# Decode attention over two layers: each batch row through both layers in turn, part of its V kept in SBUF, 0.5 MB chunks

## Chip, cores, metric

The kernel runs on one core of a Trainium2 chip. The time is that of the whole execution on the device, in microseconds; lower is better. PE is the matmul engine, PEld its weight loads, DVE VectorE, ACT ScalarE, SP the engine that issues the DMAs.

## The reference

Four batch rows with one query token each go through attention over a KV cache, an FFN, and both again with the same weights and the same cache. There are 32 query heads, 8 KV heads, 8192 keys, head size 128, model width 512, FFN width 1792, all bf16.

```python
def attention(x, k_cache, v_cache, wq, wo):       # k_cache, v_cache: [4, 8, 8192, 128]
    q = (x @ wq)...                               # [4, 32, 1, 128]
    scores = einsum("bhqd,bhkd->bhqk", q, k) * 128 ** -0.5
    return einsum("bhqk,bhkd->bhqd", softmax(scores), v)... @ wo
def ffn(x, w_gate, w_up, w_down):
    return (silu(x @ w_gate) * (x @ w_up)) @ w_down
x = x + attention(layernorm(x)); x = x + ffn(layernorm(x))
x = x + attention(layernorm(x)); x = x + ffn(layernorm(x))
```

K and V are 67.1 MB each, and both layers read both: 268.4 MB. The weights are 13.9 MB. Nearly all of the work is to read the cache.

## The kernel before

All four rows go through layer 1 together, then through layer 2. A K chunk is 1 MB: 1024 keys of one KV head for the four rows. PE transposes it in 32 blocks, DVE and ACT copy the result out of PSUM, and eight score matmuls follow. After the softmax come the V chunks. Loads are issued by SP in order, each when its buffer is free. In the K stages four 1 MB slots serve in turn (chunks 4 to 6 of a layer go to three of V's buffers besides). V has seven 1 MB slots of its own, four of them in the room of wq.

```python
def dma_k(i):                                     # 4 slots; chunks 4 to 6 in V's buffers
    src = A_k_cache[:, g, c*SR:(c+1)*SR, :].rearrange("b (p t) d -> p b (t d)", p=P)
    T.dma("sp", dst, src, sm, writes=[key])
wqr_aps = [wq_sb[:, j, :].rearrange("p (b m) -> p b m", b=B) for j in range(KT)]
vslot_aps = [vbuf[:, j, :, :] for j in range(NSV)] + wqr_aps    # V's 7 slots: 3, and wq's room
# ... cut ...
def k_loop():
    for i in range(HEAD - 1): qk(i)
    for i in range(HEAD, nchunks):
        transposes(i)                             # 32 transposes, 4 evacuations, next load
        qk(i - 1)                                 # 8 score matmuls; softmax block after 8 heads
    qk(nchunks - 1)
# ... cut ...
def prefetch_vk():                                # called for layer 2 only
    for i in VK: dma_k(i)
    if not last:                                  # layer 2 is the last one: never true here
        T.dma("sp", wq_sb[:], A_wq..., sem_w["wq"], writes=["wq"] + wqr_keys)
# ... cut ...
L1["qproj"](); L1["qpad_fill"](); ...; L1["k_loop"](); L1["finalize_pt"]()
L1["pv"](next_layer=L2); L2["prefetch_vk"](); L1["residual"]()
ffn_up(); ffn_act(final=False); ffn_down(); ...   # a few K chunks of layer 2 stand between
L2["qproj"](); ...; L2["k_loop"](); L2["finalize_pt"](); L2["pv"](next_layer=None)
```

## Time and profile before

735.52 us (median of 4 runs, 735.38 to 736.36).

| what | value | view |
|---|---|---|
| bytes loaded | 282.35 MB | queue table |
| DMA rate in most slices | 400 to 408 GB/s | slices |
| time for the bytes at 408 GB/s | 692 us | worked out |
| span less that time | 43 us | worked out |

First the page: busy times, then the span in 40 equal slices (busy tenths of PE, granted clock of PE in tenths, rate of DMA), the queue of the loads, and the chain of work that ended last.

```profile
PE 512.5 (70%) x10040; PEld 387.3 (53%) x10040; DVE 281.1 (38%) x494; ACT 237.8 (32%) x293; POOL 1.6 (0%) x11
...
PE   2999999999644444444489999999996444444444
...
PEclk9999999999755555555569999999997655555555
...
GB/s 340 405 406 406 404 405 404 407 388 398 398 408 406 407 407 406 407 407 407 411 379 327 312 406 405 406 405 404 403 401 369 400 407 408 407 406 406 408 358 1
...
q1 hardware_dynamic: 142688, 282.35, 100.0%
...
DMA 48%; PE 28%; SPq 17%; DVE 4%; issue 2%; ACT 0%; ACTq 0%; DVEq 0%
```

DMA is near its best rate in all but a handful of slices, whether PE is full (K stages) or half idle (V stages). That is a DMA-bound kernel. The chain agrees: DMA and its issuing queue are two thirds of it.

Then windows of the trace: start and end, length, busy time of each engine, granted clock, DMA share, GB/s. They are a K stage, a V stage, the layer boundary and the tail.

```profile
40.00:200.00 160.00, 148.48 (x2351) 114.44 (x2348) 110.04 (x178) 101.34 (x126) 0.00 (x0) 0.97 1.05 401
225.00:330.00 105.00, 49.21 (x1333) 33.43 (x1321) 5.67 (x15) 0.00 (x0) 0.00 (x0) 0.57 1.05 407
...
390.00:410.00 20.00, 18.00 (x301) 13.95 (x298) 13.79 (x25) 11.54 (x15) 0.00 (x0) 1.00 0.76 287
...
715.00:735.00 20.00, 9.34 (x233) 6.57 (x222) 5.91 (x16) 2.00 (x4) 0.00 (x0) 0.50 0.02 7
```

PE is 93% busy in the K stage while DMA still runs at 401 GB/s. So K work only just fits behind its loads. The timeline of PE shows by how little (start, duration, operation):

```profile
66.61 1.96 PE L369 MATMUL ps<-ident,kraw 128*128 128x128 bf16 x32
68.50 0.61 PE L419 MATMUL ps<-ktp,qpad 128*32 128x512 bf16 x8
69.09 1.96 PE L369 MATMUL ps<-ident,kraw 128*128 128x128 bf16 x32
```

From one chunk to the next are 2.48 us here (2.44 at best), and 1 MB at 408 GB/s takes 2.57.

The issue list has SP's issues of loads into wq's room:

```profile
wq_sb<-in_A_v_cache_dram SPq DMA_DIRECT2D x72, 1024.0 KB, 13.6
...
wq_sb<-in_A_wq_dram SPq DMA_DIRECT2D x1, 4096.0 KB, 12.4
```

wq is loaded once, and V chunks are then written over it, in layer 1 too. So the kernel before forms layer 2's queries from V data. The comparison with the reference does not see it: computed on a CPU in fp32 from the reference and its inputs (not a run of the record), the attention output has an rms of 0.000046 beside 2.4 in the result, and replacing wq by V data or by zeros in layer 2 leaves the largest difference from the reference at 0.084 in all cases. Leaving attention out altogether gives 0.079. So "correct" in this document says nothing about the attention of any kernel; for that there is only the reading of the code.

### The profile page before, as it was taken

Reading aid. Unit: us, or ns where it says so; the run is one execution under the profiler, and the core shown is the slowest. Engines: PE = TensorE matmul, PEld = TensorE weight load, DVE = VectorE, ACT = ScalarE, POOL = GpSimd, SP = SyncE. Lnnn points to the kernel's source line nnn. Section 1 sums busy time; section 2 is a strip of 40 time slices with the busy share of each in tenths; the row PEclk is TensorE's granted clock in tenths of the full one; section 3 lists DMA queues with packets and bytes.
Section 4 is the critical chain, followed back from the end, with each engine's and each line's share of the span. In section 5 each row is a group of like instructions: output and inputs, shape, how many; then the busy total and the mean of one; then the engine's idle time right before and its main releaser. Section 6 shows DMA issues by size and latency. Waiting matters only on the chain.

```text
span 734.9 us, 21945 instructions
## 1 busy us (share of the span) xinstructions
PE 512.5 (70%) x10040; PEld 387.3 (53%) x10040; DVE 281.1 (38%) x494; ACT 237.8 (32%) x293; POOL 1.6 (0%) x11
## 2 busy tenths in 40 slices
PE   2999999999644444444489999999996444444444
PEld 2877677767532333333277777777775333332333
DVE  2676667766500000000135776677664000000003
ACT  1566566656500000000044666666664000000001
POOL 0000000000000000000000000000000000000000
PEclk9999999999755555555569999999997655555555
DMA  8999999999999999999998999999999999999990
GB/s 340 405 406 406 404 405 404 407 388 398 398 408 406 407 407 406 407 407 407 411 379 327 312 406 405 406 405 404 403 401 369 400 407 408 407 406 406 408 358 1
DMA packets 142780, 283.75 MB, mean 386 GB/s; under 512 B 4184, under 2 KB 10080, under 8 KB 142176
## 3 DMA queue, kind: packets, MB, share of 16 engines
q1 hardware_dynamic: 142688, 282.35, 100.0%
q8 instruction: 78, 1.28, 0.6%
q14 instruction: 14, 0.11, 0.0%
HBM read 282.33 MB, written 0.00 MB: 384 GB/s over the span
## 4 chain that ended last, share of the span: by engine, by line
DMA 48%; PE 28%; SPq 17%; DVE 4%; issue 2%; ACT 0%; ACTq 0%; DVEq 0%
DMA kraw<-in_A_k_cache_dram 24%; PE ps L369 17%; SPq L92 17%; DMA vbuf<-in_A_v_cache_dram 13%; DMA wq_sb<-in_A_v_cache_dram 10%; PE ps L419 4%; PE ps L518 3%; PE ps L500 2%; DVE ktp L292 1%; DVE o_red L487 1%; PE ps L472 1%; PE ps L338 0%; PE ps L567 0%; DVE pp L464 0%; DVE o_accb L492 0%
## 5 line engine op out<-in xcount | busy, mean ns | idle before, releaser
L369 PEld LDWEIGHTS ps<-ident,kraw 128*128 128x128 bf16 x3904 | 224.7, 99 | 62.4 <-DMA kraw<-in_A_k_cache_dram 58.8
L369 PE MATMUL ps<-ident,kraw 128*128 128x128 bf16 x3904 | 245.5, 223 | 11.0 <-DMA kraw<-in_A_k_cache_dram 8.4
L292 DVE COPY ktp<-ps 128x1024 bf16<-128x1024 bf16 x310 | 207.1, 688 | 97.2 <-PE ps L369 97.2
L294 ACT ACTIVATE ktp<-ps 128x1024 bf16<-128x1024 bf16 x186 | 183.7, 1021 | 127.8 <-PE ps L369 127.8
L518 PE MATMUL ps<-wq_sb,pp 128*32 128x128 bf16 x2304 | 76.0, 294 | 84.1 <-DMA wq_sb<-in_A_v_cache_dram 84.1
L487 DVE TENSOR_REDUCE o_red<-ps 128x128 f32<-128x384 f32 x16 | 8.9, 558 | 295.7 <-PE ps L518 295.7
L518 PEld LDWEIGHTS ps<-wq_sb,pp 128*32 128x32 bf16 x2304 | 55.8, 130 | 102.0 <-DMA wq_sb<-in_A_v_cache_dram 92.9
L306 ACT ACTIVATE sdv<-mv,eps_sb 4x1 f32<-4x1 f32 x4 | 1.2, 294 | 334.9 <-DVE mv L305 334.9
L518 PE MATMUL ps<-vbuf,pp 128*32 128x128 bf16 x1792 | 59.6, 296 | 66.3 <-DMA vbuf<-in_A_v_cache_dram 65.8
L518 PEld LDWEIGHTS ps<-vbuf,pp 128*32 128x32 bf16 x1792 | 43.6, 130 | 80.3 <-DMA vbuf<-in_A_v_cache_dram 70.9
L419 PE MATMUL ps<-ktp,qpad 128*32 128x512 bf16 x992 | 78.7, 385 | 4.7 <-DVE ktp L292 2.2
L500 PE MATMUL ps<-wo_sb,oT_sb 128*4 128x512 bf16 x64 | 29.9, 622 | 5.1 <-DVE oT_sb L498 5.1
L419 PEld LDWEIGHTS ps<-ktp,qpad 128*32 128x32 bf16 x992 | 17.2, 94 | 22.1 <-DVE ktp L292 7.1
L408 ACT ACTIVATE pp<-ps,negm 128x512 bf16<-128x512 f32 x32 | 22.0, 687 | 8.4 <-DVE negm L404 5.3
L404 DVE TENSOR_REDUCE negm<-ps 128x1 f32<-128x512 f32 x32 | 20.6, 686 | 3.4 <-PE ps L419 3.4
L472 PE MATMUL ps<-ident,pp 128*128 128x128 bf16 x128 | 14.4, 314 | 8.6 <-DVE pp L464 7.1
L472 PEld LDWEIGHTS ps<-ident,pp 128*128 128x128 bf16 x128 | 13.3, 149 | 10.1 <-DVE pp L464 8.1
L292 DVE COPY pp<-ps 128x1024 bf16<-128x1024 bf16 x20 | 13.4, 689 | 10.6 <-PE ps L369 5.4
L495 PE MATMUL ps<-ident,o_accb 128*128 128x128 bf16 x16 | 4.6, 289 | 16.7 <-DVE o_accb L492 14.8
L294 ACT ACTIVATE pp<-ps 128x1024 bf16<-128x1024 bf16 x12 | 12.1, 1022 | 12.4 <-PE ps L369 6.7
L500 PEld LDWEIGHTS ps<-wo_sb,oT_sb 128*4 128x4 bf16 x64 | 5.6, 108 | 17.5 <-issue 9.5
L495 PEld LDWEIGHTS ps<-ident,o_accb 128*128 128x128 bf16 x16 | 1.7, 104 | 21.0 <-DVE o_accb L492 18.5
(60 smaller groups left out, 120.5 us busy)
## 6 DMA issues: line engine op xcount, KB each, us to landing
kraw<-in_A_k_cache_dram SPq DMA_DIRECT2D x122, 1024.0 KB, 8.2
wq_sb<-in_A_v_cache_dram SPq DMA_DIRECT2D x72, 1024.0 KB, 13.6
vbuf<-in_A_v_cache_dram SPq DMA_DIRECT2D x56, 1024.0 KB, 13.6
vbuf<-in_A_k_cache_dram SPq DMA_DIRECT2D x6, 1024.0 KB, 14.1
wq_sb<-in_A_wq_dram SPq DMA_DIRECT2D x1, 4096.0 KB, 12.4
wo_sb<-in_A_wo_dram SPq DMA_DIRECT2D x1, 4096.0 KB, 18.7
wg_sb<-in_B_w_gate_dram SPq DMA_DIRECT2D x1, 1792.0 KB, 15.3
wu_sb<-in_B_w_up_dram SPq DMA_DIRECT2D x1, 1792.0 KB, 17.3
```

Source lines behind the costliest of these rows:

```text
L92: ins = self.eng[engname].dma_start(out_ap, in_ap)
L292: T.op("dve", lambda e: e.tensor_copy(dst, src), reads=reads, writes=writes)
L294: T.op("act", lambda e: e.activation(dst, src, ACTF.Copy), reads=reads, writes=writes)
L369: T.op("pe", lambda e: e.matmul(stg[:, t * P:(t + 1) * P], lhsT=kap[:, b, t * Dh:(t + 1) * Dh], rhs=ident[:], is_transpose=True, start=Tru ...
L404: T.op("dve", lambda e: e.tensor_reduce(negm[:, k:k + 1], scb, AX.X, ALU.max, negate=True), reads=[f"pb{bank}"], writes=[f"negm{k}"])
L408: T.op("act", lambda e: e.activation(pp[:, k * 512:(k + 1) * 512], scb, ACTF.Exp, bias=negm[:, k:k + 1], scale=1.0, accum_out=lsum[:, k:k ...
L419: T.op("pe", lambda e: e.matmul(ps[32 * b:32 * (b + 1), bank * BANKF:(bank + 1) * BANKF], lhsT=qpad[:, b, g, :], rhs=src[:, q2 * 512:(q2 + ...
L472: T.op("pe", lambda e: e.matmul(stg[:, t * P:(t + 1) * P], lhsT=pp[:, blk * P:(blk + 1) * P], rhs=ident[:], is_transpose=True, start=True, ...
L487: T.op("dve", lambda e: e.tensor_reduce(o_red[:], src, AX.X, ALU.add), reads=keys, writes=["ored"])
L495: T.op("pe", lambda e: e.matmul(misc_bf[:, 0:P], lhsT=o_accb[:], rhs=ident[:], is_transpose=True, start=True, stop=True), reads=["oacc", " ...
L500: T.op("pe", lambda e: e.matmul(ps[0:B, OPJ * BANKF:(OPJ + 1) * BANKF], lhsT=oT_sb[:, bass.ds(h, B, step=Hq)], rhs=wo_sb[:, h, :], start=( ...
L518: T.op("pe", lambda e: e.matmul(ps[32 * b:32 * (b + 1), bank * BANKF: bank * BANKF + Dh], lhsT=pp[:, blk * P + 32 * b: blk * P + 32 * (b + ...
```

## The change

The intent is to load less. If one row goes through layer 1 and at once through layer 2, a part of its V can stay in SBUF for layer 2. Ten of the row's 32 V chunks are kept (0.5 MB each, one row, 2048 keys of one head). The FFN of layer 1, the query projection of layer 2, their norms and the output projection of layer 1 then run once per row instead of once for all four, interleaved with score work of the next row. (The first query projection and the last FFN stay common to all rows.) wq stays in SBUF for good, as do the other weights. The norm uses Ln and Exp instead of Sqrt.

```diff
-    SR = 1024            # 1 MB chunks: all four rows
-    NSK = 4; NSV = 3
+    CR = 2048            # 0.5 MB chunks: one row
+    NRING = 7            # ring slots for K and V chunks
+    NRET = 10            # kept V chunks
...
+        kept_ix = {}                              # the first ten of a row's V chunks
+        for g in range(G):
+            for c in range(NCH):
+                if len(kept_ix) < NRET:
+                    kept_ix[(g, c)] = len(kept_ix)
...
+        LATE = [4, 5, 6, 7]
+        phases = [("A1", 0, A_of(0, 0, range(NCH)))]                       # K of row 0, layer 1
+        for b in range(B):
+            ahead = A_of(0, b + 1, (0, 1)) if b + 1 < B else []
+            phases.append(("B1", b, merge(B_of(0, b, range(G)), ahead)))   # V layer 1 + K of next row
+            fill = A_of(0, b + 1, (2, 3)) if b + 1 < B else B_of(1, b - 1, LATE)
+            phases.append(("C1", b, fill))                                 # FFN + K of next row
+            phases.append(("A2", b, A_of(1, b, range(NCH))))               # K layer 2
+            gs = [g for g in range(G) if not (b == B - 2 and g in LATE)]
+            phases.append(("B2", b, B_of(1, b, gs)))                       # V layer 2
...
+            T.op("act", lambda e: e.activation(lnv[:], mv[:, 1:2], ACTF.Ln, bias=eps_sb[:], scale=1.0), ...)
+            T.op("act", lambda e: e.activation(rstd[:], lnv[:], ACTF.Exp, scale=-0.5), ...)
...
+                attn_residual(x0, "x0"); ln_dve(); some(2); ln_T(); some(1)    # stage C1:
+                ffn_up(); some(3); ffn_down(); some(1); ffn_out()              # some(n): n chunks
+                ln_dve(); some(3); ln_T(); some(1); q_proj(); q_fill(...); some(len(units))
```

Below, "mixed stage" is C1 (FFN and chunks), "K stage" is A2, and the V stages are B1 and B2.

## The prediction

> **What bounds the kernel now.** The page's slices show DMA at 400 to 408 GB/s almost throughout; the queue table has 282.35 MB. At 407 GB/s that is 694 us of the 735. The rest: 2.7 us before the first byte, about 18 us of tail (windows: 715 to 735 us moves 7 GB/s), and the layer boundary (390 to 410 us: 287 GB/s). K and V stages differ. In the K stage PE is also nearly full: 148 of 160 us busy; in the timeline a 1 MB chunk with data waiting takes 2.44 us (32 transposes 1.89, 8 score matmuls 0.55), its transfer 2.58. In the V stage PE is half idle. So before is DMA-bound, with K work just fitting, and about 7 MB of buffers ahead.
>
> **What the change removes.** The second load of wq (4.2 MB), and for layer 2 ten of each row's 32 V chunks (40 x 0.52 = 21 MB): 261 MB, 643 us at 407 GB/s. About 52 us fewer, an estimate from bytes.
>
> **What it adds and moves.**
> - The FFN, norms and projections run once per row, not once per layer: about 8.4 us of small matmuls each (3.3 up, 1.6 down, 3.4 q-projection, from the timeline), plus 32 output projections per row instead of per layer (29.9 us for 64 before, at half clock).
> - Per row, 16 K chunks mixed with that work, then 32 K chunks alone, then softmax, then ten kept V chunks. A K chunk should need 1.25 us of PE (half of 2.44 plus some overhead) against 1.29 us of DMA: no reserve to catch up.
> - The norm uses Ln and Exp. The instruction order shows two table loads in each; a load took 1283 ns here (the Trainium skill, "ScalarE activation tables", gives the same), inside the chain.
> - Finalization with transposes and the row-weight chain: about 9 us of PE waiting per row and layer (before: 13 us with 64 transposes).
> - Lookahead in the ring shrinks to seven 0.5 MB slots, 9 us.
>
> **Critical path.** For rows 0 to 2, PE from the end of layer-1 V to the first ring release in layer-2 V: mixed stage about 37 us, K stage 43, finalization 9, kept chunks 7 (releasing no slot): about 96 us. DMA can use about 70 (54 chunks), so it idles about 27 us per row. For row 3 about 18. Sum about 100 us of DMA idle, more than the 52 saved. The interleaved V stages stay roughly DMA-bound (7.7 us per group against 7 to 8 of PE).
>
> 643 + 3 + 20 + 100 = **766 us**; I predict **768**, range **728 to 815**. Faster by over 2%: **0.10**; within 2%: **0.18**; slower: **0.72**.
>
> **What would show it.** Bytes near 261 MB (right if so). GB/s near 405 in the interleaved V stages, with three or four dips, each beginning in the mixed stage and deepest when layer-2 V starts. SP's longest waits on PE transposes and kept-V matmuls. PE busy above 90% in the 32-chunk K stages at 1.25 us per chunk. Tail about 20 us. Eight to ten norms with two table loads each.
>
> **What would make it wrong.** If K chunks take 1.2 us and the chains hide behind them, idle falls to 60 us and the time to about 730. If the clock drops through the small matmuls (the boundary before had 0.67; the Trainium skill, "TensorE: Matmul & The Clock Gate", Part 1, says low activity halves it, and the V stages' 0.54 agree), mixed chunks take up to twice as long: 790 and more. If 4 KB rows move faster than 407 GB/s, less.

## The result, and the profile after

822.34 us (median of 4 runs, 819.2 to 823.19): 1.117 times the time before (95% interval 1.114 to 1.120). The result is correct. A ratio is the mean time of one kernel's fast runs over that of the other's in the same rounds, so it is not quite the ratio of the medians. The direction was predicted (slower); the time is outside the stated range, 54 us above the central value.

The page after, with the lines that answer to those of before:

```profile
PE 611.3 (74%) x11140; PEld 438.8 (53%) x11140; DVE 334.7 (41%) x705; ACT 258.1 (31%) x323; POOL 0.7 (0%) x6
...
PE   3876767788975667689896476678898666699664
...
PEclk9999799889996599878897569977899687599776
...
GB/s 359 386 395 407 392 409 404 265 198 260 379 291 270 409 408 408 353 193 238 226 396 156 386 409 408 408 258 194 237 331 349 278 408 392 267 391 374 127 378 8
...
q1 hardware_dynamic: 75584, 261.40, 84.1%
...
PE 46%; DMA 32%; DVE 7%; SPq 7%; ACT 5%; issue 3%; ACTq 0%; DVEq 0%
```

The bytes are as predicted: 261.40 MB, 21 MB less. But DMA has four valleys, one per row, and the chain's largest share is now PE. At 408 GB/s the bytes take 641 us, so DMA loses 181 us of the 821, in which it stands still or moves less, against 43 before. This loss is called its idle below. That is 138 us more idle for 51 us less load, together the 87 us that the span grew.

The windows below follow row 0 from the end of its layer-1 V: the interleaved V stage before it, the mixed stage, the K stage of layer 2, the finalization of its softmax, the kept V chunks, the restart of DMA, and the rest of layer 2's V.

```profile
84.80:147.60 62.80, 44.50 (x826) 28.35 (x826) 17.61 (x36) 13.05 (x14) 0.00 (x0) 0.89 1.03 402
147.60:188.90 41.30, 34.53 (x626) 27.52 (x624) 20.08 (x38) 18.74 (x25) 0.00 (x0) 0.83 0.64 217
188.90:236.70 47.80, 43.92 (x664) 33.14 (x660) 33.19 (x61) 28.69 (x35) 0.00 (x0) 1.00 0.92 344
236.70:245.10 8.40, 3.14 (x29) 1.78 (x29) 5.24 (x18) 3.11 (x6) 0.00 (x0) 0.85 0.49 192
245.10:252.00 6.90, 5.50 (x219) 4.77 (x223) 1.56 (x6) 0.00 (x0) 0.00 (x0) 0.69 0.07 8
252.00:256.00 4.00, 1.68 (x89) 1.15 (x77) 0.52 (x2) 0.00 (x0) 0.00 (x0) 1.00 0.75 247
256.00:280.00 24.00, 12.32 (x276) 7.62 (x276) 2.71 (x9) 0.00 (x0) 0.00 (x0) 0.50 1.03 410
```

Length times (1 - rate/408) is DMA's idle in a window: 19.3, 7.5, 4.4, 6.8 and 1.6 us from the mixed stage to the restart, together 39.6. The last window shows that nothing is wrong with the 0.5 MB loads themselves: as soon as slots come free, DMA moves 410 GB/s. The same sum is 45 us for row 1, 40 for row 2 and 26 for row 3, about 151 in all. Start and tail lose about 24 us more.

The kernel before has a finalization too, in layer 1 from 186 to 200 us, and DMA goes on at 399 GB/s in that window, against 192 here. V has slots of its own there, and SP begins to issue loads into them at 175.6 us. After the change one ring serves both K and V.

What DMA waits for is in the waits of SP's queue (who waited for whom, us in total, times, longest), before and then after:

```profile
SPq L62 <- PE ps L369: 249.8, 108, 12.0
...
SPq L62 <- PE ps L518: 9.9, 7, 8.6
```

```profile
SPq L62 <- PE ps L363: 359.8, 232, 12.0
SPq L62 <- PE ps L474: 168.5, 107, 17.0
```

SP waits for PE in both kernels, so the waits alone do not tell the two apart; the rates do. After, SP's longest wait is for a V matmul, 17 us, twice what the seven ring slots hold (3.7 MB, 9 us).

Three places of PE's timeline in row 0 show where PE's own time went. The first is the beginning of the mixed stage. The number in brackets is the idle time before, and what ended it:

```profile
153.67 0.59 PE L379 MATMUL ps<-ktp,qpad 128*32 128x512 bf16 x4 [4.13 <-DVE ktp L240]
154.20 0.26 PE L522 MATMUL ps<-ident,xn_bf 4*128 4x4 bf16 x4
154.39 1.89 PE L363 MATMUL ps<-ident,ring 128*128 128x128 bf16 x16
```

PE stood still for 4.13 us. The evacuation that it names was queued on DVE behind the last step of the norm, which waited for ACT. And 16 transposes then took 1.89 us, against 1.07 in the K stage:

```profile
186.28 1.07 PE L363 MATMUL ps<-ident,ring 128*128 128x128 bf16 x16
187.28 0.40 PE L379 MATMUL ps<-ktp,qpad 128*32 128x512 bf16 x4
187.61 1.07 PE L363 MATMUL ps<-ident,ring 128*128 128x128 bf16 x16
```

In the K stage a chunk takes 1.33 us, where the prediction had 1.25. The third place is the end of the K stage:

```profile
240.39 1.18 PE L425 MATMUL ps<-ident,pp 128*128 128x128 bf16 x16 [2.14 <-DVE pp L410]
...
244.27 0.58 PE L458 MATMUL ps<-one,rowl 1*128 1x1 f32 x2 [2.47 <-DVE rowl L454]
245.10 1.90 PE L474 MATMUL ps<-kept,pp 128*32 128x128 bf16 x64 [0.25 <-DVE wrow L461]
```

PE waits for the rescaling of the scores, then for a chain of seven small operations that makes the row weights, and only then starts on V.

### The profile page after: what moved, and what is told of

Same layout as the page of the kernel before. It is cut to its first block, busy times and chain, and to the rows that moved or that the text cites. A ratio compares the mean times of both kernels' runs of the same rounds, so it can differ in the third digit from the quotient of the medians.

```text
span 821.4 us, 24777 instructions
## 1 busy us (share of the span) xinstructions
PE 611.3 (74%) x11140; PEld 438.8 (53%) x11140; DVE 334.7 (41%) x705; ACT 258.1 (31%) x323; POOL 0.7 (0%) x6
## 3 DMA queue, kind: packets, MB, share of 16 engines
q1 hardware_dynamic: 75584, 261.40, 84.1%
## 4 chain that ended last, share of the span: by engine, by line
PE 46%; DMA 32%; DVE 7%; SPq 7%; ACT 5%; issue 3%; ACTq 0%; DVEq 0%
PE ps L363 24%; DMA ring<-in_A_k_cache_dram 16%; DMA ring<-in_A_v_cache_dram 15%; PE ps L379 8%; SPq L92 7%; PE ps L474 5%; PE ps L530 2%; PE ps L548 2%; DMA wq_sb<-in_A_wq_dram 2%; PE ps L501 2%; ACT L515 1%; DVE ktp L240 1%; ACT pp L393 1%; DVE negm L391 1%; PE ps L425 1%
## 5 line engine op out<-in xcount | busy, mean ns | idle before, releaser
L363 PE MATMUL ps<-ident,ring 128*128 128x128 bf16 x4096 | 301.3, 233 | 32.2 <-DMA ring<-in_A_k_cache_dram 31.7
L363 PEld LDWEIGHTS ps<-ident,ring 128*128 128x128 bf16 x4096 | 255.7, 104 | 83.6 <-issue 41.6
L379 PE MATMUL ps<-ktp,qpad 128*32 128x512 bf16 x1024 | 117.7, 420 | 27.5 <-DVE ktp L240 25.3
L474 PE MATMUL ps<-ring,pp 128*32 128x128 bf16 x2816 | 95.8, 254 | 53.0 <-DMA ring<-in_A_v_cache_dram 51.1
L474 PEld LDWEIGHTS ps<-ring,pp 128*32 128x32 bf16 x2816 | 57.3, 108 | 82.2 <-DMA ring<-in_A_v_cache_dram 72.4
L483 DVE TENSOR_SCALAR o_g<-ps,wrow 128x128 bf16<-128x128 f32 x64 | 22.4, 350 | 144.8 <-PE ps L474 144.8
L501 PE MATMUL ps<-wo_sb,oT 128*4 128x512 bf16 x160 | 54.6, 476 | 0.5 <-DVE oT L496 0.5
L474 PE MATMUL ps<-kept,pp 128*32 128x128 bf16 x1280 | 43.0, 280 | 6.3 <-DMA kept<-in_A_v_cache_dram 2.7
L474 PEld LDWEIGHTS ps<-kept,pp 128*32 128x32 bf16 x1280 | 30.0, 123 | 14.4 <-DMA kept<-in_A_v_cache_dram 6.5
L530 PE MATMUL ps<-xnT,wq_sb 128*128 128x4 bf16 x640 | 17.4, 165 | 6.0 <-DMA wq_sb<-in_A_wq_dram 6.0
L458 PE MATMUL ps<-one,rowl 1*128 1x1 f32 x16 | 4.3, 332 | 20.1 <-DVE rowl L454 20.1
```

The costliest lines, as they stand in the source:

```text
L363: T.op("pe", lambda e: e.matmul(stg[:, t * P:(t + 1) * P], lhsT=ap[:, blk * Dh:(blk + 1) * Dh], rhs=ident[:], is_transpose=True, start=Tru ...
L379: T.op("pe", lambda e: e.matmul(ps[32 * j:32 * (j + 1), bk * BW:(bk + 1) * BW], lhsT=qp, rhs=ktp[:, s, (j % 2) * 512:(j % 2 + 1) * 512], s ...
L474: T.op("pe", lambda e: e.matmul(ps[32 * j:32 * (j + 1), bk * BW:bk * BW + Dh], lhsT=pp[:, q, (c * NM + m) * P + 32 * j:(c * NM + m) * P + ...
L483: T.op("dve", lambda e: e.tensor_scalar(o_g[:, og, :], ps[:, bk * BW:bk * BW + Dh], wrow[:, q:q + 1], None, op0=ALU.mult), reads=[f"pb{bk} ...
L501: T.op("pe", lambda e: e.matmul(ps[0:B, OPJ * BW:OPJ * BW + D], lhsT=oT[:, l, h, :], rhs=wo_sb[:, h, :], start=(h == 0), stop=(h == Hq - 1 ...
L530: T.op("pe", lambda e: e.matmul(misc[:, h * B:(h + 1) * B], lhsT=wq_sb[:, kt, h * Dh:(h + 1) * Dh], rhs=xnT[:, kt * B:(kt + 1) * B], start ...
```

## The experiments

**Theory.** From the end of a row's layer-1 V to the first slot that layer 2's V gives back, PE's work is longer than what DMA can load meanwhile: K chunks give no time back (1.33 us of PE for 1.29 us of load), and the FFN, norms, finalization and kept chunks come on top. The ring of 3.7 MB fills, and DMA stands still. **Rivals.** The 0.5 MB loads are slower; or the added work hides behind the chunks, and only the total of PE work or of bytes counts.

All kernels gave a correct result, with the limit that was said above. The runs were made in sets on several chips; in every set the kernel before had a median between 735.5 and 736.9 us. The changed kernel was run in the first set only. Runs of one kernel lie up to 10 us apart here, the longer ones mostly at a lower mean clock (e4: 801.02 us at 0.844, 811.17 at 0.832), so a few us between two medians decide nothing.

### Nothing kept, the room given to the ring (e1)

```diff
-    NRING = 7
-    NRET = 10
+    NRING = 17
+    NRET = 0
```

> Changed kernel with no V kept: the 10 kept slots become ring slots (17 instead of 7), so layer 2 loads all its V again (282.4 - 4.2 = about 278 + 4 = 282.4 - wq once: 282.4 MB less 0; i.e. 261.4 + 21.0 = 282.4 MB, 51 us more of DMA). Theory (DMA stands still because a row's stretch of K work outruns the lookahead): 10 more slots let DMA work 13 us longer per row, and the first V chunks of layer 2 release slots at once (7 us per row), so about 79 us of idle go and 51 us of load come: about 794 us. Rival (what is kept is worth its bytes; the stalls have nothing to do with lookahead): 822 + 51 = 873 us.

807.84 us (801.97 to 810.49), with 282.37 MB. 21 MB more are loaded, and the kernel is 14 us faster. The rival is out by 65 us; the theory's number is missed by 14. In the profiled run (801.97 us) the idle is 108 us instead of 181. That is 73 us less, where 79 were expected. Two of its windows answer to the mixed stage and to the kept chunks of row 0:

```profile
147.90:190.80 42.90, 36.12 (x636) 28.82 (x634) 20.04 (x39) 19.49 (x25) 0.00 (x0) 0.76 0.88 330
...
247.10:254.00 6.90, 5.48 (x233) 4.83 (x237) 1.56 (x6) 0.00 (x0) 0.00 (x0) 0.73 0.69 258
```

DMA moves 330 GB/s instead of 217, and 258 instead of 8. The V kept in SBUF costs more, as ring slots that are missing and as chunks that give no slot back, than its bytes save. The run does not separate these two.

### The last ten V chunks kept instead of the first (e2)

```diff
-        for g in range(G): ...                    # the first NRET
+        for n in range(G * NCH - NRET, G * NCH):
+            kept_ix[(n // NCH, n % NCH)] = len(kept_ix)
-        LATE = [4, 5, 6, 7]
+        LATE = [0, 1, 2, 3]
```

> Same bytes kept, but the last ten V chunks of a row instead of the first ten, so that layer 2's V starts with chunks whose slots go back to the ring. Theory: the 7 us of V work per row that release nothing move from just after the softmax (DMA standing still) to the end of the stage: 4 x 7 = 27 us less, about 795 us. Rival (which chunks are kept does not matter, only how many): 822 us.

816.66 us (813.68 to 822.5): 6 us in the medians, not 27, and the ranges overlap, so a gain is not shown. The profiled run is the slowest, 822.5 us. Its rates hint at a reason; the valley of row 0 is slices 8 to 14:

```profile
GB/s 361 385 396 407 388 408 409 263 187 262 379 304 374 347 410 408 314 200 235 209 388 243 412 354 409 409 234 192 262 382 287 341 409 330 246 391 372 215 295 3
```

Slices 12 and 13 rise from 291 and 270 to 304 and 374, and slice 14 falls from 409 to 347. This fits the reading that ten chunks in a row that give no slot back cost something wherever they stand, and that the expectation took a move for a removal. No further run tests it.

### The norm without tables, by Newton steps (e3)

```diff
-   activation(lnv, var, Ln, bias=eps); activation(rstd, lnv, Exp, scale=-0.5)
+   vv = var + eps; rstd = bits(1597463007 - (bits(vv) >> 1))                  # on DVE
+   three times: yy = rstd * rstd; yy = yy * vv * -0.5; rstd = (yy + 1.5) * rstd
```

> The norm's Ln and Exp on ScalarE, with two table loads each time, replaced by a reciprocal square root by Newton steps on VectorE: no table load after the first. Theory (the norm chains are on the path of the mixed stage): 3 to 5 us per row, about 805 to 812 us. Rival (they hide behind the interleaved K chunks, as the change intended): 822 us.

826.25 us (823.49 to 827.11), no gain but 4 us more. The experiment did not test its point: twelve operations of 0.14 to 0.20 us on DVE were nearly as long a chain (2.3 us in the trace) as DVE's wait for ScalarE had been (2.6 us, in which the tail of one table load, the other load and two activations stand). PE waited 3.89 us there instead of 4.13.

### The row-weight matmul later in PE's order (e4)

```diff
-            bk2 = next_bank()
-            T.op("pe", ... lhsT=rowl[:], rhs=one1[:] ...)
+            delayed.append((2, lambda: row_column(q)))      # the same matmul, two chunks later
```

> The row-weight matmul, which waits for a chain of seven small operations, is put two chunks later in PE's order. Theory: the waits of 2.4 us in the K stage (rows 0 to 2) and at its end (all rows) go: 7 x 2.4 = 17 us, about 805 us. Rival (PE has slack there): 822 us.

805.92 us (801.02 to 811.17), 16 us less; 17 expected. PE's waits for the row weights fall from 20.1 to 4.6 us in all. One matmul per row and layer, placed where PE has to wait for its input, cost 2% of this kernel.

### The norm as before, with Sqrt (e5b)

```diff
-   activation(lnv, var, Ln); activation(rstd, lnv, Exp, scale=-0.5)
+   activation(lnv, var, Sqrt); activation(dmy, one1, Exp); reciprocal(rstd, lnv)
+   # and before attn_residual and after ffn_up: activation(dmy, one1, Sqrt), to load its table
```

> The norm as the kernel before has it: Sqrt, its table loaded ahead, and a reciprocal on VectorE (the Newton version turned out to be as long a chain, 2.3 us against 2.6, and did not test the point). Theory: both norm chains of the mixed stage lose their table loads, PE's waits of 4.1 and 2.7 us there shrink to about half: 3 to 4 us per row for rows 0 to 2, about 810 us. Rival (norms hidden): 822 us or above.

811.63 us (810.66 to 813.19), as expected. PE's wait at the beginning of row 0's mixed stage falls from 4.13 to 2.82 us. The norm was not hidden.

### Score matmuls of two K chunks together (e6b)

```diff
-                prev, pending[:] = list(pending), [(u, hv)]
-                for x in prev: k_back(*x)
+                pending.append((u, hv))
+                if len(pending) == 3:
+                    prev, pending[:] = pending[:2], pending[2:]
+                    for x in prev: k_back(*x)
```

> Score matmuls of two K chunks back to back (8 in a row, as before) instead of 4 after every chunk. Theory: a K chunk takes PE 1.22 us (as in the kernel before) instead of 1.33, because each switch between transposes and score matmuls costs about 0.05 us on both sides; 48 chunks a row in the stretch where DMA waits for PE: 3 x 5 + 3 = 18 us, about 804 us. Rival (the chunk time is set by the evacuations, not by PE's switches): 822 us.

803.46 us (801.16 to 808.92). PE's timeline in this kernel:

```profile
207.15 1.96 PE L363 MATMUL ps<-ident,ring 128*128 128x128 bf16 x32
209.04 0.61 PE L379 MATMUL ps<-ktp,qpad 128*32 128x512 bf16 x8
209.58 1.96 PE L363 MATMUL ps<-ident,ring 128*128 128x128 bf16 x32
```

2.43 us for two chunks, 1.22 each as before, against 1.33. In neither timeline does PE wait for an evacuation within these chunks, so the rival is out. The difference is the cost of alternating between the two kinds of matmul twice as often, which the smaller chunk brought.

### Another order: V chunks beside the FFN (e7b)

```diff
-            fill = A_of(0, b + 1, (2, 3)) if b + 1 < B else B_of(1, b - 1, LATE)
+            fill = A_of(0, 1, (2, 3)) if b == 0 else B_of(1, b - 1, LATE)
-            gs = [g for g in range(G) if not (b == B - 2 and g in LATE)]
-            phases.append(("B2", b, B_of(1, b, gs)))
+            gs = [g for g in range(G) if not (b < B - 1 and g in LATE)]
+            beside = A_of(0, b + 1, (2, 3)) if 0 < b < B - 1 else []
+            phases.append(("B2", b, merge(B_of(1, b, gs), beside)))
-    NRET = 10
+    NRET = 9                                       # and a third score buffer
```

> The order of work changed, nothing else: the FFN of row 1, 2 and 3 is interleaved with late V chunks of the row before (cheap on PE), and the K chunks that stood there go beside the early V chunks of layer 2. A third score buffer takes the place of one kept slot (9 instead of 10, 2 MB more). Theory (idle comes from K chunks, FFN and finalization standing in one stretch): the idle of rows 1 and 2 falls from about 40 us to about 25 or less, about 790 us. Rival (the total of PE work decides, not its order): 827 us.

795.48 us (793.12 to 801.1), with 2 MB more. The idle of the whole profiled run (801.1 us, the slowest) is 154 us instead of 181; that of rows 1 and 2, which the theory names, was not measured by itself. But for the kept slot and the score buffer the work is the same, only its order differs. So the total of PE work is not what binds; where it stands is.

### The kernel before with 0.5 MB loads (e8b)

```diff
+    for lo in (0, 2):                              # two rows per load, one semaphore per slot
+        dma_start(out_ap[:, lo:lo + 2, :], in_ap[:, lo:lo + 2, :]).then_inc(sem, 16)
```

> The kernel BEFORE with each 1 MB load split in two of 0.5 MB. Theory (chunk size itself costs nothing): 735 us, DMA at 405 GB/s. Rival (0.5 MB loads are slower): each of 270 chunks costs up to 0.5 us more, 800 us or above.

735.55 us (734.84 to 735.83), ratio 0.998. The size of the loads is not a cause. (The longer pieces in which the changed kernel reads, 4 KB per row of SBUF, are not in this run; that they are not slower is shown by the 410 GB/s above.)

### The parts together (c1, c2)

c1 is e4, e5b, e6b and e7b in one kernel. c2 adds six K chunks of the next row in the gap before layer 2's V:

```diff
-            phases.append(("A2", b, A_of(1, b, range(NCH))))
+            phases.append(("A2", b, A_of(1, b, range(NCH)) + gap))    # gap: 6 chunks of K(0, b + 1)
```

> Four parts that each helped, together: row weights later (-16), norm by Sqrt (-11), paired score matmuls (-19), V chunks beside the FFN (-27). If the losses are one chain on which each adds its part: 822 - 73 = 749 us. If they overlap (each hides the same idle of DMA): 770 us or above.

761.43 us (760.2 to 763.41). 61 of the 73 us add up.

> The same, and six K chunks of the next row put between layer 2's last K chunk and its first V chunk (rows 0 to 2), so that PE has work while the softmax is finalized. Theory: the 5 to 6 us in which PE waits there go, in three rows: 16 us less than the four parts alone, about 733 us. Rival: the six chunks merely move, no gain.

753.31 us (752.02 to 755.2): 8 us, half of what was expected.

### Fewer kept chunks in that version (c3, c4)

> As the one before, with 4 kept chunks and 12 ring slots instead of 9 and 7. 10.5 MB more (26 us), 5 chunks more lookahead (6.4 us per row) and a shorter stretch of kept chunks (3 us per row): if lookahead still is what lacks, -38 + 26, 12 us less than with 9 and 7, about 720 us; if the other parts have removed the idle, 26 us more, about 758 us.

744.11 us (743.72 to 745.72), 273.98 MB.

> As the one before, with nothing kept and 16 ring slots. 18.9 MB more than with 9 kept (46 us). DMA time 284 MB / 407 = 693 us, with start and tail 716 us; if lookahead then hides all other waits, 720 to 730 us, below the kernel before because wq is loaded once; if not, 750 us or above.

737.5 us (736.16 to 740.38), 282.37 MB. From 9 to 4 to 0 kept chunks, bytes rise and time falls. (The remark on wq in this expectation is wrong: the kernel before loads it once too.)

### The small matmuls doubled (x1)

```diff
-                ffn_up() ... ffn_down() ... q_proj()
+                ffn_up(2) ... ffn_down(2) ... q_proj(2)      # in the mixed stage, each matmul twice
```

> The changed kernel with every FFN and q-projection matmul of the mixed stages done twice (same result). Theory (they stand in the stretch where DMA waits for PE): 8.4 us more per row in rows 0 to 2, a little less in row 3 where V chunks stand beside them: 26 to 32 us more, about 850 us. Rival (hidden behind the loads): 822 us.

860.17 us (856.28 to 863.3): 38 us more, above the 26 to 32 expected. The matmuls that were added are about 34 us long (four times 8.4), so on the whole none of this work is hidden. The two profiled runs are 33 us apart, and the transposes at the end of the K stage show where it arises: about 12, 9, 4 and 8 us in rows 0 to 3.

### What was left in the combined version (x2, x3, x4)

```diff
-  some(2) ... some(1) ... some(3) ... some(1) ... some(3)    # rows 1 and 2
+  some(5) ... some(1) ... some(4) ... some(1) ... some(4)
-  delayed.append((0, o_select)); one PSUM bank for V
+  delayed.append((1, o_select)); two banks in turn
+  row 3: eight V chunks of row 2 between its last K chunk and its own V
```

> The combination with the gap (9 kept, 753 us), and three things more: five instead of two V chunks ahead of each norm, the head selection one chunk later with a second PSUM bank for V, and V chunks of row 2 in the gap before the last row's V. Theory: 3 to 4 us in rows 1 and 2 and 6 to 8 us in row 3: about 739 us. Rival (what is left is not in these waits): 753 us.

744.43 us (743.03 to 745.98).

> The same with 4 kept and 12 ring slots: 744 - 12 = 732 us if the waits were what was left. Keeping pays only if this or the one with 9 kept beats the one with none.

735.6 us (733.79 to 736.58); ratio to the kernel before 0.998, not different from it.

> The same with nothing kept and 16 ring slots: 737 - 8 = 729 us; its floor is 284 MB / 408 = 696 us plus 22 of start and tail.

737.1 us (735.77 to 737.35), the same as without these additions: it is close to DMA-bound, as its slices show. With 4 kept, 8.4 MB less (21 us at 408 GB/s) bring 1.5 us, and the ranges overlap; with 9 kept it is slower again. Keeping V does not pay in any version tried.

```profile
GB/s 354 388 388 409 399 399 409 408 408 294 385 406 322 402 407 408 408 407 408 408 401 407 407 406 409 408 407 409 406 390 395 408 408 408 371 377 400 391 403 12
```

### The kernel before with wq loaded for layer 2 (y1)

```diff
-                if not last:
-                    T.dma("sp", wq_sb[:], A_wq..., writes=["wq"] + wqr_keys)
+                T.dma("sp", wq_sb[:], A_wq..., writes=["wq"] + wqr_keys)    # ahead of the VK loads
```

> The kernel before with wq loaded again ahead of layer 2's queries (its condition never loads it a second time). 4.2 MB more at 407 GB/s: 10 us, if DMA-bound there too, about 746 us, with 286.5 MB read. If the load delays the queries beyond the data it is queued with: 750 us or above. Rival (the layer boundary has slack for it, DMA is at 287 to 330 GB/s there): 736 to 740 us.

747.98 us (747.03 to 748.28), ratio 1.016. Against this version, which computes what the reference says, x3 and x4 are about 1.7% and 1.5% faster (ratios of medians from different sets; under the 2% at which runs here are called faster), and the change is 9.9% slower. No version was found that beats the kernel before as it stands.

The idle in the table is the span of the profiled run less its bytes at 408 GB/s:

| kernel | us | MB | kept | idle, us |
|---|---|---|---|---|
| before | 735.5 | 282.4 | - | 43 |
| before, wq loaded twice (y1) | 748.0 | 286.6 | - | 43 |
| changed | 822.3 | 261.4 | 10 | 181 |
| four parts (c1) | 761.4 | 263.5 | 9 | 113 |
| and the gap (c2) | 753.3 | 263.5 | 9 | 104 |
| and x2's additions | 744.4 | 263.5 | 9 | 97 |
| the same with 4 kept (x3) | 735.6 | 274.0 | 4 | 62 |
| the same with none (x4) | 737.1 | 282.4 | 0 | 44 |

## Why the prediction was right in direction and wrong in size

**Right.** The bytes (261 MB, but see below), the saving of about 52 us, the mechanism (DMA idle in every row, from the mixed stage to layer 2's V), the finalization (9 us predicted, 8.4 in row 0) and the kept chunks (7, 6.9). e1, e4, e5b, e6b, e7b and x1 each move the time in the direction that the mechanism says, and e8b excludes the size of the loads.

**The step that failed** is the sum under "Critical path": "so it idles about 27 us per row. For row 3 about 18. Sum about 100 us". The trace has 40, 45, 40 and 26, about 151: these 51 us are nearly all of the 54 that the central value missed. In row 0 the terms were mis-sized so:

| term | predicted us | measured us |
|---|---|---|
| mixed stage | 37 | 41.3 |
| K stage | 43 | 47.8 |
| finalization | 9 | 8.4 |
| kept chunks | 7 | 6.9 |
| loads that DMA did meanwhile | 70 | 66.3 (27.1 MB) |
| restart | 0 | 1.6 |
| idle | 27 | 39.6 |

- *K stage.* "A K chunk should need 1.25 us of PE" was half of a 1 MB chunk and a little more. It took 1.33. e6b shows that the difference is the alternation of transposes and score matmuls: pairing them gives 1.22 and 19 us. The prediction had counted operations and not how often their kind changes. In row 0 this makes 2.6 of the 4.8 us (32 times 0.08, an estimate). The rest was not taken apart, but the next row's softmax of layer 1 is finalized in this stage, with waits of 1.47 and 2.41 us, beside the one finalization that the sum counts.
- *Mixed stage.* Sixteen chunks at 1.33 and 8.0 us of small matmuls make 29.3 us, PE's two waits behind the norms 6.8 (4.13 and 2.65). An estimate of about 5 us is left for chunks at half clock and the rest. The norm waits alone would have fitted into the predicted 37; the clock is what was left out. The prediction did name the clock, as a case that would make it wrong ("790 and more"), and left it out of the central value and nearly out of the range. The trace has a clock of 0.83 and 0.76 in the mixed stages of rows 0 and 1, and 16 transposes at 1.89 us. In row 1 the K stage itself ran at 0.94 and took 53.1 us. What lowers the clock was not tested by a run of its own: in row 0 two of the four stretches at half clock begin after the norm waits (at about 153.7 and 174.2 us) and two after streams of small matmuls (160.7 and 181.1).
- *Loads meanwhile.* 54 chunks assumed, about 52 measured, for a reason that was not looked into. Full rate returned only after the four windows (247 GB/s in the 4 us of the restart).

**Also wrong:** "The second load of wq (4.2 MB)" is not in the kernel before; it was read from the code's intent. With it the sum would be 257 MB. The 261 came out right because the 4.2 MB were named and then not subtracted, which is luck. And the "7 MB of buffers ahead" hold for the V stages alone; the K stages before had four slots, 4.2 MB, hardly more than the ring of 3.7.

**What stays open.** c1 gives 61 of 73 us and c2 half of its 16; which of the parts hide the same idle was not taken apart. In x2 about 75 us of idle remain besides start and tail (742.6 us span, 646 at 408 GB/s, about 22 of tail and slow first slices).

## What to carry to other kernels

A DMA-bound kernel pays for every stretch in which no buffer comes free and which is longer than what its buffers hold; buffers that keep data are buffers taken from the lookahead, and keeping is worth its bytes only if the stretch still fits. Before trading bytes for order, add up the consumer's longest stretch between two releases, with its waits, its clock and its changes of operation, and compare it with the bytes that fit ahead. Work that ran once per layer and now runs once per row is not hidden by interleaving it with chunks that already need the whole engine; put it beside chunks that leave the engine idle.

## What the Trainium skill lacked or had wrong

- "ScalarE: Activation LUTs", section "Table sets: the hidden batching unit", says that Ln then Exp need one table load, since one set has both. Here 10 norms had 20 loads, one for each Ln and one for each Exp (1283 ns each); some of those for Ln were done before its input was ready (row 0's second norm: at 165.9, Ln at 169.9 us). The section "What ACT_TABLE_LOAD costs" gives about 2.66 us for a switch, a drain of 1.38 us included; in the trace the Exp load began 0.02 us after the Ln ended, took 1.28 us, and Exp began 0.02 us later, so this switch cost 1.32 us. "ScalarE activation tables: per-element evaluation and per-set limits", section "What a function is on this engine", gives 1283 ns, which agrees.
- "DMA: Bandwidth & Descriptors", section "Rules for kernel authors", asks for at least 1 MiB per DMA for full bandwidth. With loads queued one behind the other, 0.5 MB did as well: 735.55 us, 0.998 of the kernel before in the same set (e8b), and 410 GB/s after the change. The page does not say whether its rule is meant for a load by itself or for one of many in a queue.
- "TensorE: Matmul & The Clock Gate", Part 1, describes the halved clock, and the trace agrees (16 transposes at 1.89 and 1.07 us). It does not say what a stream of matmuls of 4 columns, about 26 ns apart, does to the clock. Here the clock fell to 0.5 at about the end of the q-projection's stream in each of rows 0 to 2 (3.2 us of matmuls from 177.6, 369.9 and 568.0 us; low from about 181, 372 and 570), and after the 1.5 us of ffn_down it did not. Whether the stream is the cause was not tested.
- "TensorEngine Tiling (Array Packing)", section "Key Properties", says that a change of tiling mode drains the engine, but neither it nor another page gives a time for going between full-array transposes and 32-column score matmuls. Here a chunk took 1.33 us when they alternate every 16 transposes, and 1.22 when every 32 (e6b).
